# Second MoE of a fused attention and two-MoE kernel: the input-side products on two PSUM banks, zeroed by writing, one output sum in their upper halves

## Chip, cores and metric

One NeuronCore of a Trainium2 chip runs the whole program in one launch. The metric is the device time of an execution in microseconds (us). Five engines work side by side and meet only through semaphores: TensorE (PE) multiplies, VectorE (DVE) and ScalarE (ACT) do element-wise work and read PSUM, GpSimd (POOL) does element-wise work between SBUF tiles, and SyncE (SP) issues the DMAs. PSUM, into which PE writes, has eight banks; a tile of 128 x 512 fp32 values fills one.

## The reference, cut to what matters

```python
scores = q @ k.T * scale                      # 4 x 8 heads, 576 x 576
attn = softmax(where(scores >= max - tau, scores, -1e9))
x = (attn @ v), heads side by side            # 2304 x 512
h = x @ w1_in                                 # 512 -> 2048
x = (h * clip(h + 3, 0, 6) / 6) @ w1_out      # first MoE, 2048 -> 512
h = x @ w2_in
out = (h * sigmoid(1.702 * h)) @ w2_out       # second MoE
```

## The kernel before

The program keeps tokens on the free axis and features on partitions. Every fp32 operand is split into two numbers of a shorter format, a high and a low one, and a product is three matmuls: high by high, high by low, low by high. Attention and the first MoE come first (to about 659 us of the profiled execution), then the second MoE, which is where the diff works.

**The second MoE.** `moe2` (L1368) takes a block of 512 tokens (four of them) or of 256 (one, called `whole`). The feed-forward width is cut into eight pairs of 128 x 2; two sweeps (`q` = 0, 1) take four pairs each over all blocks, the first sweep storing its sums in DRAM, the second adding to them. One block and one pair are called a step here: 40 steps, 32 of them with 512 tokens. A step of 512 tokens uses a 2 x 2 scheme with seven products in place of eight, on the input side (`hidden2`, L1251, matmuls at L1269) and on the output side (`yout` and `prod` in `moe2`, matmuls at L1395). One product is six matmuls with 256 columns. A step of 256 tokens has four products on each side.

- Input side: the seven products go to the two 256-column halves of one PSUM bank (`ps`, class 3 of `bank`, of which one may be open). Each half is a running sum that is never started anew within the step; after some products ACT copies the running value out (`kept`: tiles p1, p5, u2 and half of b) or DVE adds it to such a copy (`plus`). The two results a and b (128 x 512 each) are made of these and one subtraction between SBUF tiles (`TC`, on DVE or POOL).
- Between: `gate2` (L1313) applies a sigmoid on ACT (L1338), a multiplication on DVE, four differences, and splits the results into high and low parts (ACT copies, then differences on DVE or POOL: tiles g and gl).
- Output side: the seven products of a step add to seven sums that live over the four pairs of a sweep; four of them are the `py` banks and three are banks of `pm`, class 4. At the end of a block the sums are combined on DVE and POOL and stored.

The order of all instructions is not the order of the code. `Plan` collects operations with their costs; `order` (L221) schedules them by a table of ranks (`RANKS`), with the number of open banks per class in `CAPS`, and another table (`SWAPS`) says which operations with two possible engines take the second one. Each engine then runs its instructions in that order. A wait is made wherever two instructions touch the same tile. In the time that the plan leaves PE idle, `fill` (L361) puts matmuls on a constant tile (`busy`, L1566).

Lines in the profile: L507 is the ACT copy helper, L510 the two-input element-wise helper on DVE or POOL, so those are told apart by their tiles. `pm` is any of the four banks of that pool, `xhxs`/`xlxs` and many `inhring`, `outhring` tiles hold activations.

Of the kernel before, what the change touches and what calls it, by code (L numbers as in the profile page):

```python
# [15 lines left out]
ALU = mybir.AluOpType  # L16
# [15 lines left out]
CAPS, BANKS, LANES = (2, 2, 3, 1, 3), 4, 8  # L32
# [4 lines left out]
3jhuP4gnqk3IJLFM*sx^J^|nXq5)0;9RmFU0s%PzegQB6H~|s?t^qs&YynFFR{>K2K>;cOi~)23QUOT;ZUJ%uX8~9ND*?~}DFHwMpaEI|NCDab`vHvsf&pFulL1Tt6afYS!U049M*-piv;k=W(g8{V8UcU-Q3A68s{vF2`~l7Z;{h20?*WPd  # L37
p8}`>uK_gzsR4!o3IYoPdjZS=RsjS8K?3Lj_W^4GSOV|?g8{4oA_8UtSpl#CrvZEc8UmyNhXD}+B?9&V>H$jvTLJ<C5&}B{6#{btVFGXhtO9QWS^`G`Ujj@57y>H-b^?L|4FV(rRswPY1_EFL2m;pu3<Ko?ya53M+XC1DECQ_ofdTgb^#NZ2
+yVaqnF3+~kpT|@-~iSD*Z__I3;`wqNdou)mH@5*p8$;jSpYczdI1pu@&V=m(E!c>#Q>-Ph5&s47XY6D3;+cHwE!gnZUAQh9RL~t0RU(Khyi8+Z2^4&cmbIKj{#)?i2(or8vrf<2>=5CCID3cNdQ~`H2?wtBLG+c761qU9{_X!e*l00PXH$X
TLCcuVF7Xg$N+}`<Nz`N`~Y15gaMTSAOgw(k^vk6w*lV)bpgEr-T|fo=>Y%%WC1n-&jA4e4FLlI%>X|ER{}%=2?EgpodMJVJp!BojsXM!sQ}*qaR6fgGyqEg!vH}5Isj7u-2k!xwg8d<Bmf}*EdVS45&+r&Kmy?akO86q%>j=9xB*rGE&|X1  # L40
# [6 lines left out]
C<CDa76VuVTLY&8q66v!DFinIaRXHY&;ykN&jYpt<O96}=L2*E$^(}J^aBb62L#Cj_XBtXCIrp{3k2H)W(1!EF$5k2e*~BWR0L53ZUlS;_5-~HV+6Paf&?D~X9TeXfCRe*O9k-+t^_Uwa|Db8sRVuor34cN00p)LmIQbNVg#KAItA_oHw8om
T?H5g!UQ}82L%QNs07&r%><MLTm|?FV+$Dz(ggklV+Aq={RBk?Z3RLFItywG{t9;mqXmKmg$0QP?FDWH<OOXDmkc`#u?2$#(FJ=2D+Uh+M+S}s><U5)WD86KWCFzjQUd(~+W~F@jRNljr~)ekz5>VsGy<3c$OF;>aRT!KmI7S@GXwquZ~zbl
#sa(oP67-9YXkHGpaVJs4g-?|dIKK=`2uYN+W<TRO#_1mIRo<mu>&Fln+5U$R0C)OGy}8)cLUi2U;~8%rUP;V#{+u<M+1ukz5|W}m;>$u5d^aX#{otI>H_})_yR)%`~q+T*aA2MNCSBTAOnp9N&`*<^8>;Ir31ACfdktE*#M^lsRMljqysJk
fCFO#ECYuFh65l3W&@l9g9E<<Zvz4ZngbdHMFT7Zr~~2yKm;TNp##GM@&nWZVgr!_mIDt3*aX%D-2?&!9tHUX>;xbMQUxsoDFeU)4+A>``U2(x4FgL96a!rYSpzBq1p`R~ZUYwsbpyKtuLHFN-vep`4+J&?90Q&MUIX0&%>&B=?E{hn-~-hI  # L50
90bt=c?7ZpsspD4gacs%w*ycEF9eJO1O(Ru^#khz1q8VR`UB$wH3TaJ83afKCj^oNJ_Jt$RRp&LWdtJxy9DV2>;otS{{zGW7X;`7Lj<q`I|PUW!2{9*lmm$bnFHnnhXhFkFa!exiv+j>aRlT9TLggwJp<kYX#@ZSpafO~6a+T}Jp@Mtn*^Bz
lLU1H#sqc*&jeWn`UI;4qy)eNQUrzs)CAlF2?RU@X9d&+>;+W?{RNE$Uj?BBs|BD1`va>3Uju&wj|2Dv76e8FdIVkseFQ25Oaxj4d;>ECT?BFjO9UkZ;RG86f&(-J76niQ8w9EZZv?Ugkpy1^;{-VbIs`ifjRfrkAq1iXU<8i@a0EmIECmb&
=md@gVFbwpx&+q*Aq5Bp$^@JQWCYU$^#m6M`vgY?Fa<pYZv|NeKLs%b`~$oM9R=b9Qv`PeDg`11Y6MCIgapF`Nd@)<1_Xly{{&VAv;^=390gznA_RT}k_8n6G6X*aZ3ImO4Ft>sQv)yqQUeVIB?a^Z5(H5N;RA{VN(FQUCj}4%Qw1gkfCUu=
X$AKLe+4!LF9qublLg@g00zDV=>^CI3kIMDG6xt0bOX!;djyaK<pekc-vsysXaqC`4h16x#01C$?*u3Xzy#(5vjn6CSOrc5g#=dx+5`&)odog(DFx&L9RunF^8`!<Km{2EwFLtO5e47`qXYy6CIi9(MFc_wuLAr8K?Ga`p#*jXl?A2*#{{ec
5(Pm8=LAp%O$EjUWd#8Rlm#;dcm;?Az69$8bp^!(z5#gwiUeu_E&;;=?g5knS_1_E@dNM!uLR2k&;+mqVg>R5;sEXd?*ME7_5i;C=m6>fi~vIbGXUHGi33{ziUW86S_O6hvjs5$Bn4>z><9D!aRCYgx&=Q2mIXcq`T%nPssPLe9|u+kcK}xa
X$SrWss<<rPyjmt5CNM3+XZL_j|Hj)-UJ2)`2}?b%mtkVzy;C;odW>`Q3gT==LP5mdIlc`Mh1iiJqAGr9tQjctp)G}7zQ#15e6Fut_2eYzXntWBnFTMX$HXtuLa=-Rt9(m3<g97QU){z0tO)lBL-&%KnA1+bOwJ0Wd_Lxe+QxlZU!y}lm=V|
# [325 lines left out]
def tile_top_attention_moe_moe2(  # L382
# [76 lines left out]
    def buf(tag, ring, pool, shape, dt=F32):  # L459
        return Buf(pl, tag, ring, lambda: pools[pool].tile(shape, dt, tag=tag, name=tag, bufs=ring), pool)  # L460
# [743 lines left out]
    def halves(c0, n, whole, K):  # L1204
# [425 lines left out]
```

## Time and profile before

| | |
|---|---|
| median of 3 runs | 1101.16 us (1095.71 to 1102.01) |
| the profiled execution: its own time | 1096.64 us |
| its span | 1094.8 us |
| busy over the span: PE, weight loads, DVE, ACT, POOL | 95%, 87%, 83%, 60%, 49% |

The profile is of one execution. Its engines' busy times overlap. A matmul's duration includes its way through the array, so the next one starts before the last has ended, and PE's pace is read from the distance between starts. An idle time is named by what ended it.

### The profile page before, as it was taken

Reading aid. Unit: us, or ns where it says so; the run is one execution under the profiler, and the core shown is the slowest. Engines: PE = TensorE matmul, PEld = TensorE weight load, DVE = VectorE, ACT = ScalarE, POOL = GpSimd, SP = SyncE. Lnnn points to the kernel's source line nnn. Section 1 sums busy time; section 2 is a strip of 40 time slices with the busy share of each in tenths; the row PEclk is TensorE's granted clock in tenths of the full one; section 3 lists DMA queues with packets and bytes.
Section 4 is the critical chain, followed back from the end, with each engine's and each line's share of the span. In section 5 each row is a group of like instructions: output and inputs, shape, how many; then the busy total and the mean of one; then the engine's idle time right before and its main releaser. Section 6 shows DMA issues by size and latency. Waiting matters only on the chain.

```text
span 1094.8 us, 21058 instructions
## 1 busy us (share of the span) xinstructions
PE 1038.8 (95%) x7564; PEld 956.1 (87%) x7564; DVE 905.3 (83%) x1845; ACT 653.8 (60%) x1307; POOL 536.3 (49%) x641
## 2 busy tenths in 40 slices
PE   8999999999999999999999998999999879888998
PEld 6687878899988889999999997988988878888898
DVE  7999999988998957878878776777898999778865
ACT  5898776767776646664544445555556845444452
POOL 3688887866485626554653433343423121433332
PEclk9999999999999999999999999999999999999999
DMA  7334457777866654456458772142315631211202
GB/s 233 106 111 144 143 160 221 201 196 197 247 204 189 177 163 131 146 189 197 142 171 285 224 254 82 49 150 83 107 44 183 217 110 46 78 58 59 87 11 78
DMA packets 98633, 160.70 MB, mean 147 GB/s; under 512 B 9056, under 2 KB 61408, under 8 KB 96480
## 3 DMA queue, kind: packets, MB, share of 16 engines
q1 hardware_dynamic: 98384, 159.06, 47.9%
q8 instruction: 60, 0.98, 0.4%
q14 instruction: 45, 0.37, 0.1%
q10 hardware_dynamic: 144, 0.29, 0.1%
HBM read 106.76 MB, written 52.56 MB: 146 GB/s over the span
## 4 chain that ended last, share of the span: by engine, by line
PE 72%; DVE 12%; DMA 6%; ACT 5%; issue 3%; POOL 2%; SPq 1%; DVEq 0%; ACTq 0%; POOLq 0%
PE pm L1269 15%; PE py L1073 8%; PE py L1395 8%; PE pm L1048 8%; PE pm L1163 6%; PE pm L1073 5%; PE ps L768 5%; PE pm L1395 4%; PE pm L986 4%; PE pm L894 3%; DVE c L510 2%; PE pm L970 2%; DMA wrawstg<-in_w1o_dram 2%; PE ps L808 1%; ACT p L507 1%
## 5 line engine op out<-in xcount | busy, mean ns | idle before, releaser
L824 DVE TENSOR_REDUCE nm<-ps 128x1 f32<-128x576 f32 x144 | 105.6, 748 | 16.6 <-PE ps L768 12.0
L507 ACT ACTIVATE g<-t 128x256 fp32r<-128x256 f32 (+3 forms) x178 | 86.4, 489 | 44.2 <-DVE t L510 20.3
L827 ACT ACTIVATE e<-ps,nm 128x576 f32<-128x576 f32 x128 | 92.4, 736 | 28.6 <-DVE nm L824 24.1
L1073 PE MATMUL pm<-g,outhring 128*128 128x256 f32 (+1 forms) x512 | 106.4, 300 | 0.0
L828 DVE SCALAR_TENSOR_TENSOR e<-ps,th,e 128x576 f32<-128x576 f32 x128 | 102.0, 809 | 3.8 <-ACT e L827 1.9
L1073 PE MATMUL py<-g,outhring 128*128 128x432 f32 (+2 forms) x384 | 97.1, 337 | 1.8 <-DVE yc L510 1.0
L510 POOL TENSOR_TENSOR g<-t,g 128x256 fp32r<-128x256 f32 (+2 forms) x74 | 66.4, 898 | 66.0 <-ACT g L507 44.8
L1048 PE MATMUL pm<-xh,inhring 128*128 128x256 f32 (+1 forms) x320 | 96.9, 303 | 0.4 <-DVE t L1060 0.3
L1048 PE MATMUL pm<-xh,inlring 128*128 128x256 f32 (+1 forms) x320 | 94.6, 296 | 0.0
L1048 PE MATMUL pm<-xl,inhring 128*128 128x256 f32 (+1 forms) x320 | 94.5, 295 | 0.0
L768 PE MATMUL ps<-kqv 128*128 128x288 f32 x480 | 81.6, 302 | 1.2 <-DVE kqv L510 0.5
L1073 PEld LDWEIGHTS pm<-g,outhring 128*128 128x128 f32 x512 | 82.0, 190 | 0.6 <-issue 0.5
L510 POOL TENSOR_TENSOR wmstg<-wmstg,wrstg 128x512 uint32<-128x512 uint32 x40 | 55.1, 1380 | 53.1 <-DVE wmstg L564 39.8
L1073 PE MATMUL pm<-g,outlring 128*128 128x256 f32 (+1 forms) x256 | 75.9, 297 | 0.0
L768 PEld LDWEIGHTS ps<-kqv 128*128 128x128 f32 x480 | 68.4, 190 | 8.0 <-issue 3.9
L1073 PEld LDWEIGHTS py<-g,outhring 128*128 128x128 f32 x384 | 68.6, 188 | 4.2 <-DVE yc L510 1.2
L510 DVE TENSOR_TENSOR t<-t,c 128x512 f32<-128x512 f32 (+1 forms) x80 | 57.3, 723 | 16.3 <-ACT t L1338 15.7
L510 DVE TENSOR_TENSOR g<-t,g 128x256 fp32r<-128x256 f32 (+2 forms) x86 | 52.2, 610 | 15.2 <-ACT g L507 14.5
L1073 PE MATMUL py<-g,outlring 128*128 128x432 f32 (+2 forms) x192 | 64.7, 337 | 0.0
L510 POOL TENSOR_TENSOR kqv<-qk,kqv 64x576 fp32r<-64x576 f32 (+1 forms) x40 | 57.8, 1444 | 11.7 <-ACT kqv L507 4.7
L897 ACT ACTIVATE et<-pm 128x512 f32<-128x512 f32 (+2 forms) x102 | 55.2, 557 | 13.5 <-PE pm L894 12.6
L1048 PEld LDWEIGHTS pm<-xh,inhring 128*128 128x128 f32 x320 | 60.6, 189 | 1.1 <-PE pm L1571 0.5
(245 smaller groups left out, 3704.4 us busy)
## 6 DMA issues: line engine op xcount, KB each, us to landing
turned<-tr SPq DMA_DIRECT2D x16, 1024.0 KB, 4.4
et<-turned SPq DMA_DIRECT2D x64, 256.0 KB, 5.6
wrawstg<-in_w1i_dram SPq DMA_DIRECT2D x16, 512.0 KB, 4.0
wrawstg<-in_w1o_dram SPq DMA_DIRECT2D x16, 512.0 KB, 3.7
wrawstg<-in_w2i_dram SPq DMA_DIRECT2D x16, 512.0 KB, 4.3
wrawstg<-in_w2o_dram SPq DMA_DIRECT2D x16, 512.0 KB, 4.4
qk<-in_q_dram SPq DMA_DIRECT2D x24, 288.0 KB, 4.5
qk<-in_k_dram SPq DMA_DIRECT2D x24, 288.0 KB, 4.2
```

What stands on the lines that cost most here:

```text
L507: return lambda: nc.scalar.activation(out=o(), in_=i(), func=ACTF.Copy, **kw)
L510: return lambda: (nc.vector if eng == DVE else nc.gpsimd).tensor_tensor(out=o(), in0=a(), in1=b(), op=op)
L768: nc.tensor.matmul(ps.t[:, i, :SH], q, w[hd].t[:, i * SH:(i + 1) * SH], start=a, stop=z)
L824: add(DVE, 672, K("R", s), "R", lambda: nc.vector.tensor_reduce(out=nm.t[:, c], in_=ps.t[:, :, :SH], op=ALU.max, axis=AX.XY, negate=True), ...
L827: add(ACT, 624, K("X", s), "X", lambda: nc.scalar.activation(out=ev(), in_=ps.t[:, :, :SH], func=ACTF.Exp, bias=nm.t[:, c]), [ps, (nm, s)] ...
L828: add(DVE, 736, K("M", s), "M", lambda: nc.vector.scalar_tensor_tensor(out=ev(), in0=ps.t[:, :, :SH], scalar=th.t[:, c], in1=ev(), op0=ALU ...
L897: add(ACT, act(size), K("EH", at), "EH", lambda: nc.scalar.activation(out=dst()[0], in_=dst()[1](pt.t[row:kn, :size]), func=ACTF.Copy), [p ...
L1048: nc.tensor.matmul(ph.t[:, :n], a, v, start=(cc == 0 and i == 0), stop=(cc == KC - 1 and i == 2))
L1073: nc.tensor.matmul(py.t[:, :n], a, v, start=(st and i == 0), stop=(sp and i == 2))
L1163: nc.tensor.matmul(ph.t[:, :n], a, v, start=(cc == 0 and q == 0), stop=(cc == KC - 1 and q == 2))
L1269: nc.tensor.matmul(half(i)(), u.t[:, ws], v.t[:, xv], start=(st and kk == 0 and j == 0), stop=(sp and kk == 1 and j == 2), skip_group_chec ...
L1395: nc.tensor.matmul(o.t[:, cc * n:cc * n + n], u.t[:, ws], v.t[:, at:at + n], start=(st and j == 0 and cc == 0), stop=(sp and j == 2), skip ...
```

## The change

Two banks of `pm` are taken for good at the start of the second MoE (`pab`). Each holds, in its lower 256 columns, one of the two running places of the input side, and in its upper 256 columns half of the output sum of product (0, 0). No matmul into these banks sets the start flag; instead ACT writes zeros (`zero`: an identity tile times 0.0), over both banks once, over both lower halves after each step (40 steps, 80 writes), and over both upper halves at the end of each 512-token block (16 writes). `CAPS` lets two banks of class 3 be open and two of class 4, in place of one and three.

Inside a step the seven products alternate between the banks, in another order, and the sums are put together another way: four copies, three additions or subtractions from PSUM and now two between SBUF tiles (`side`, on DVE or POOL) in place of one. The copy of the (0, 0) output sum (512 columns) becomes two copies of 256, one from each bank. In the output products of a step (0, 0) now comes last, except in a block's last step.

`buf` gives each place of a ring its own tag and one buffer, where one tag had as many buffers as the ring has places. `RANKS` and `SWAPS` are other tables: the whole program, attention and first MoE included, is ordered anew, and some operations change engine.

```diff
-CAPS, BANKS, LANES = (2, 2, 3, 1, 3), 4, 8
+CAPS, BANKS, LANES = (2, 2, 3, 2, 2), 4, 8
...
-    23, 42, 72, 185, 212, 247, 274, 316, 350, 383, 393, 398, 429, 495, 617, 651, 661, 669, 705, 715, 737, 745, 761, 814, 825, 846, 876, 910, 932, 949, 967, 968, 972, 997, 1002, 1008,
+    62, 72, 102, 212, 226, 247, 254, 274, 298, 309, 371, 378, 388, 398, 422, 538, 551, 617, 647, 667, 786, 793, 794, 825, 856, 885, 910, 915, 920, 925, 928, 937, 947, 953, 972, 1002,
...
-        return Buf(pl, tag, ring, lambda: pools[pool].tile(shape, dt, tag=tag, name=tag, bufs=ring), pool)
+        b = Buf(pl, tag, ring, None, pool)
+        b.make = lambda: pools[pool].tile(shape, dt, tag=f"{tag}{b.idx % ring}" if ring > 1 else tag, name=tag, bufs=1)
+        return b
...
-        ps = bank(3)
...
-            return lambda: ps.t[:, 256 * i:256 * i + n]
+            return lambda: pab[i].t[:, :n]
...
-                        nc.tensor.matmul(half(i)(), u.t[:, ws], v.t[:, xv], start=(st and kk == 0 and j == 0), stop=(sp and kk == 1 and j == 2), skip_group_check=True)
+                        nc.tensor.matmul(half(i)(), u.t[:, ws], v.t[:, xv], start=False, stop=True, skip_group_check=True)
...
+        def side(o, x, y, op, rd, wr):
+            add(DVE, dve(n), K("H2") + 4500, "TC", tt(DVE, o, x, y, op), rd, [wr], (), (POOL, pool2(n), tt(POOL, o, x, y, op)))
...
-        prod(1, (4, 1), False, False)
-        kept(first(p5), 1, [p5])
-        prod(0, (5, 3), False, False)
-        kept(first(u2), 0, [u2])
-        prod(1, (2, 4), False, True)
-        plus(a, second(a), 1, u2, 1)
-        prod(0, (6, 5), False, False)
-        plus(b, second(b), 0, p5, 1)
-        prod(0, (3, 6), False, False)
-        kept(first(b), 0, [(b, 0)])
...
-        prod(0, (1, 2), False, True)
-        plus(a, first(a), 0, p1, 0)
...
+            prod(1, (1, 2))
+            kept(first(a), 1, (a, 0))
+            prod(0, (5, 3))
+            kept(first(u2), 0, u2)
+            prod(1, (4, 1))
+            comb(first(p5), 1, (first(a), (a, 0)), ALU.subtract, p5)
+            prod(0, (6, 5))
+            comb(second(b), 0, (first(p5), p5), ALU.add, (b, 1))
+            side(first(u2), first(u2), first(a), ALU.subtract, [(a, 0)], u2)
+            prod(1, (2, 4))
+            comb(second(a), 1, (first(u2), u2), ALU.add, (a, 1))
+            prod(0, (3, 6))
+            kept(first(b), 0, (b, 0))
+            side(first(a), first(a), first(p1), ALU.add, [p1], (a, 0))
+        for i in range(2):
+            zero(i, 0, n, K("H2") + 5000)
...
+        return add(ACT, act(n), time, "Z", lambda: nc.scalar.activation(out=ap(), in_=id_b.t.unsqueeze(1).to_broadcast([P, n // P, P]), func=ACTF.Copy, scale=0.0), [id_b], [pab[i]])
...
-        accs += [bank(4) for _ in range(0 if whole else 3)]
+        accs = accs if whole else [None] + accs + [bank(4) for _ in range(2)]
...
+                    to = o.t[:, cc * n:cc * n + n] if o else pab[cc].t[:, 256:512]
...
-            for q in place:
+            for q in place if whole or i == len(w) - 1 else [*list(place)[1:], (0, 0)]:
...
+        def open_():
+            for i in range(2):
+                add(ACT, act(n), t, "KP", copy(lambda i=i: side(u)()[:, i * n:i * n + n], lambda i=i: pab[i].t[:, 256:512]), [pab[i]], [u])
+                zero(i, 256, n, t)
...
+    pab += [bank(3) for _ in range(2)]
+    for i in range(2):
+        zero(i, 0, 512, t - 10000).deps.add(changed[-2][0])
```

In the built programs PE has 7112 matmuls before and after, SP 543 instructions, DVE 1703; ACT goes from 1310 to 1442 and POOL from 646 to 652.

PE's order in the second MoE, first step of the third block worked on, at the border of two input-side products (last three matmuls of one, first three of the next; the number behind `pm` tells the tile). Before:

```order
L1269 MATMUL pm_9244<-xhxs_8404,inhring1_6632 128x256
L1269 MATMUL pm_9244<-xlxs_8415,inhring1_6632 128x256
L1269 MATMUL pm_9244<-xhxs_8404,inlring1_6643 128x256
L1269 MATMUL pm_9244<-xhxs_8420,inhring1_6762 128x256
L1269 MATMUL pm_9244<-xlxs_8446,inhring1_6762 128x256
L1269 MATMUL pm_9244<-xhxs_8420,inlring1_6777 128x256
```

PE's order there now:

```order
L1271 MATMUL pm_8359<-xhxs_8398,inhring1_6637 128x256
L1271 MATMUL pm_8359<-xlxs_8419,inhring1_6637 128x256
L1271 MATMUL pm_8359<-xhxs_8398,inlring1_6648 128x256
L1271 MATMUL pm_8365<-xhxs_8409,inhring1_6732 128x256
L1271 MATMUL pm_8365<-xlxs_8420,inhring1_6732 128x256
L1271 MATMUL pm_8365<-xhxs_8409,inlring1_6755 128x256
```

Both products wrote one tile; now each writes its own.

ACT's order in the same step (copies out of `pm` into p, u, c; `g` are high parts of the gate, `t` its sigmoid). Before:

```order
L507 ACTIVATE p_9263<-pm 128x256
L507 ACTIVATE g<-t_861 128x256
L507 ACTIVATE p_9273<-pm 128x256
L507 ACTIVATE u_9283<-pm 128x256
L507 ACTIVATE wrstg_9304<-wrawstg_9240 128x512
L507 ACTIVATE yc<-py_9054 128x512
L507 ACTIVATE c<-pm 128x256
```

ACT's order there now, where `pm<-id` is a zero:

```order
L510 ACTIVATE c<-pm 128x256
L510 ACTIVATE g<-t_936 128x256
L510 ACTIVATE p_9273<-pm 128x256
L510 ACTIVATE g<-t_888 128x256
L510 ACTIVATE u_9291<-pm 128x256
L510 ACTIVATE wrstg_9320<-wrawstg_9242 128x512
L1323 ACTIVATE pm<-id 128x256
L510 ACTIVATE c<-pm 128x256
L1350 ACTIVATE t_888<-c 128x512
L1323 ACTIVATE pm<-id 128x256
```

The four copies of a step stay; two zeros have come in among them and the sigmoids.

## Rows read from the trace of the kernel before

**Rows 1.** The page: busy time by engine, and PE's granted clock in 40 slices.
```profile
PE 1038.8 (95%) x7564; PEld 956.1 (87%) x7564; DVE 905.3 (83%) x1845; ACT 653.8 (60%) x1307; POOL 536.3 (49%) x641
...
PEclk9999999999999999999999999999999999999999
```

**Rows 2.** Busy time by stage: stretch, length, then each engine's busy us.
```profile
0.00:659.00 659.00, 648.11 (x4482) 585.02 (x4483) 559.94 (x1227) 425.05 (x827) 395.66 (x524) 1.00 0.62 185
659.00:1091.00 432.00, 390.68 (x3084) 371.03 (x3082) 344.71 (x619) 228.80 (x481) 140.62 (x117) 1.00 0.28 89
```

**Rows 3.** A group at L1269: ns min/median/max, first and last start.
```profile
L1269 PE MATMUL pm<-inhring,inhring x72: 275/282/392, 659.1 to 1043.4; 128*128 128x256 f32 x72
```

**Rows 4.** A group at L1395, same columns.
```profile
L1395 PE MATMUL py<-g,outlring x160: 276/280/288, 685.0 to 1090.6; 128*128 128x256 f32 x160
```

**Rows 5.** PE's waits from 640 us on: us in total, times, longest.
```profile
PE pm L1269 <- ACT p L507: 17.2, 33, 1.2
PE pm L1269 <- ACT u L507: 9.2, 19, 0.6
PE pm L1269 <- DVE c L510: 7.9, 11, 2.0
PE pm L1269 <- ACT c L507: 1.8, 5, 0.5
```

**Rows 6.** Timeline of PE, five input-side products: first matmul of each.
```profile
726.70 0.28 PE L1269 MATMUL pm<-xhxs,inhring 128*128 128x256 f32 x1
...
727.41 0.28 PE L1269 MATMUL pm<-xhxs,inhring 128*128 128x256 f32 x1
...
728.00 0.28 PE L1269 MATMUL pm<-xhxs,inlring 128*128 128x256 f32 x1
728.75 0.39 PE L1269 MATMUL pm<-inhring,inhring 128*128 128x256 f32 x1 [0.47 <-ACT p L507]
...
730.19 0.39 PE L1269 MATMUL pm<-outhring,inhring 128*128 128x256 f32 x1 [0.47 <-ACT p L507]
...
731.64 0.39 PE L1269 MATMUL pm<-inhring,inhring 128*128 128x256 f32 x1 [0.47 <-ACT u L507]
```

**Rows 7.** Timeline of ACT over the same products: its copies out of that bank.
```profile
728.32 0.38 ACT L507 ACTIVATE p<-pm 128x256 f32<-128x256 f32 x1 [0.47 <-PE pm L1269]
...
729.75 0.38 ACT L507 ACTIVATE p<-pm 128x256 f32<-128x256 f32 x1 [0.75 <-PE pm L1269]
731.20 0.38 ACT L507 ACTIVATE u<-pm 128x256 f32<-128x256 f32 x1 [1.06 <-PE pm L1269]
```

**Rows 8.** Groups on ACT in the second MoE, by shape.
```profile
L507 ACT ACTIVATE p<-pm 128x256 f32<-128x256 f32 x72 | 27.0, 381 | 41.6 <-PE pm L1269 41.4
...
L1338 ACT ACTIVATE t<-c 128x256 f32<-128x256 f32 x16 | 6.7, 416 | 9.5 <-DVE c L510 8.8 <-DVE g L510 0.5
```

**Rows 9.** Groups on DVE in the second MoE, by shape.
```profile
L510 DVE TENSOR_TENSOR gl<-c,g 128x512 fp32r<-128x512 f32 x42 | 33.0, 789 | 1.5 <-ACT g L507 0.7 <-PE pm L1395 0.5
...
L510 DVE TENSOR_TENSOR c<-t,c 128x256 f32<-128x256 f32 x49 | 23.4, 477 | 1.1 <-POOL c L510 1.0
L510 DVE TENSOR_TENSOR g<-t,g 128x256 fp32r<-128x256 f32 x35 | 20.1, 575 | 9.3 <-ACT g L507 9.0
...
L510 DVE TENSOR_TENSOR yc<-yc,wrawstg 128x512 f32<-128x512 f32 x10 | 8.5, 849 | 0.1
```

**Rows 10.** Busy time by stretch inside the second MoE.
```profile
780.00:960.00 180.00, 159.06 (x1241) 149.69 (x1240) 159.52 (x291) 101.56 (x211) 49.12 (x39) 1.00 0.35 113
840.00:900.00 60.00, 49.34 (x378) 45.68 (x377) 55.78 (x103) 37.70 (x79) 12.16 (x9) 1.00 0.52 168
```

**Rows 11.** Timeline of DVE, two operations with two SBUF inputs.
```profile
703.48 0.96 DVE L510 TENSOR_TENSOR g<-t,g 128x256 fp32r<-128x256 f32 x1
704.36 0.41 DVE L510 TENSOR_TENSOR c<-t,t 128x256 f32<-128x256 f32 x1
```

**Rows 12.** Timeline of POOL in the same stretch.
```profile
703.03 1.12 POOL L510 TENSOR_TENSOR c<-t 128x256 f32<-128x256 f32 x1 [0.63 <-DVE t L510]
704.49 1.43 POOL L510 TENSOR_TENSOR xlxs<-xa,xhxs 128x512 fp32r<-128x512 f32 x1 [0.34 <-ACT xhxs L507]
```

More of the change, by code (lines that the diff above doesn't have):

```diff
@@ L1279, in second, with comb @@
             return lambda: x.t[:, n:2 * n]
-        def plus(t, o, i, y, reg):
-            add(DVE, dve(n), K("H2") + 4000, "U", tt(DVE, o, half(i), first(y), ALU.add), [(ps, i), y], [(t, reg)])
+        def comb(o, i, y, op, wr):
+            add(DVE, dve(n), K("H2") + 4000, "U", tt(DVE, o, half(i), y[0], op), [pab[i], y[1]], [wr])
         def kept(o, i, wr):
-            add(ACT, act(n), K("H2") + 1000, "KP", copy(o, half(i)), [(ps, i)], wr)
-        prod(0, (0, 0), True, False)
-        kept(first(p1), 0, [p1])
@@ L1302, in hidden2 @@
-        plus(a, second(a), 1, u2, 1)
-        prod(0, (6, 5), False, False)
-        plus(b, second(b), 0, p5, 1)
-        prod(0, (3, 6), False, False)
-        kept(first(b), 0, [(b, 0)])
-        sides = [first(p1), first(p1), first(b)]
-        add(DVE, dve(n), K("H2") + 4500, "TC", tt(DVE, *sides, ALU.subtract), [(b, 0)], [p1], (), (POOL, pool2(n), tt(POOL, *sides, ALU.subtract)))
-        prod(0, (1, 2), False, True)
-        plus(a, first(a), 0, p1, 0)
+            add(ACT, act(n), K("H2") + 1000, "KP", copy(o, half(i)), [pab[i]], [wr])
@@ new lines, in side @@
+        def side(o, x, y, op, rd, wr):
+            add(DVE, dve(n), K("H2") + 4500, "TC", tt(DVE, o, x, y, op), rd, [wr], (), (POOL, pool2(n), tt(POOL, o, x, y, op)))
+        prod(0, (0, 0))
+        kept(first(p1), 0, p1)
+        if whole:
+            prod(1, (6, 0))
+            prod(1, (3, 1))
+            comb(first(b), 1, (first(p1), p1), ALU.add, (b, 0))
+            prod(0, (1, 1))
+            kept(first(a), 0, (a, 0))
+        else:
+            p5, u2 = buf("p5", 1, "ct", [P, 256]), buf("u2", 1, "ct", [P, 256])
+            prod(1, (1, 2))
[12 more added lines that the diff above has]
+            side(first(a), first(a), first(p1), ALU.add, [p1], (a, 0))
@@ L1393, in mm @@
                     ws = slice(lo + cc * P, lo + cc * P + P)
+                    to = o.t[:, cc * n:cc * n + n] if o else pab[cc].t[:, 256:512]
                     for j, (u, v, at) in enumerate(((wh, gh, ho), (wh, gl, go), (wl, gh, ho))):
[L1395 to L1397 removed]
+                        nc.tensor.matmul(to, u.t[:, ws], v.t[:, at:at + n], start=(st and j == 0 and cc == 0 and o is not None), stop=(sp and j == 2), skip_group_check=True)
+            add(PE, 6 * pe(n), K("Y", i + 1) + 640 * list(place).index(q), "Y", mm, [(wh, reg), (wl, reg), (gh, hr), (gl, lr)], [o] if o else list(pab))
         def yout(i, g):
[L1400 removed]
+            for q in place if whole or i == len(w) - 1 else [*list(place)[1:], (0, 0)]:
                 prod(i, q, g, place[q], i == 0 and q != (3, 1) if whole else i == 0, i == len(w) - 1 and q != (6, 0) if whole else i == len(w) - 1)
@@ L1457, in moe2 @@
             u, v = (uv, 0), (uv, 1)
+        def open_():
+            for i in range(2):
+                add(ACT, act(n), t, "KP", copy(lambda i=i: side(u)()[:, i * n:i * n + n], lambda i=i: pab[i].t[:, 256:512]), [pab[i]], [u])
+                zero(i, 256, n, t)
         if first:
-            add(ACT, act(2 * n), t, "KP", copy(side(u), side(a1)), [a1], [u])
+            open_()
             plus(y11, a2, u)
@@ L1467, in moe2 @@
         else:
-            add(ACT, act(2 * n), t, "KP", copy(side(u), side(a1)), [a1], [u])
+            open_()
             onto(y11, u)
```

206 lines of the change are left out of this document (100 added, 106 removed), and 23 rows, old and new, of the table SWAPS.

## The prediction

> **What bounds the kernel now.** I read the page first, then busy time by stage, then PE's waits, then timelines of single products, and last the groups by shape on DVE and ACT.
>
> PE is busy 95% of the span at a granted clock of nine tenths or more in every slice, the 2.4 GHz level [rows 1]; the question is where the rest goes. By stage [rows 2], the 659 us of attention and first MoE hold 648 us of PE work: 11 us are idle. The second MoE, from 659 to 1091 us, holds 391 of 432, and "busy" flatters it, since a matmul counts its 0.28 us while the next may start after 0.12. So take starts: the input-side and output-side products run from 659.1 [rows 3] to 1090.6 + 0.28 [rows 4], 431.8 us. There are 512 products (32 steps of 14, 8 of 8). In flow one takes 0.71 us (726.70 to 727.41) [rows 6], so all take 363.5. About 68 us are lost.
>
> PE's waits name the place [rows 5]: 33 + 19 + 11 + 5 = 68 waits of input-side products for a copy or an addition that reads their bank, 36.1 us idle. The timelines show what one is. Products start at 728.75, 730.19 and 731.64 [rows 6], 1.44 us apart where flow is 0.71. ACT's copy for the product of 726.70, all of which was issued when the next began at 727.41, starts only at 728.32 [rows 7]: 0.04 us after the end (728.00 + 0.28) of the product that followed it into the other half of the same bank. So a copy waits for whatever was last issued into the bank, and the next product waits for the copy. The halves give no overlap; only another bank would. One such turnaround costs 1.44 - 0.71 = 0.73 us, of which the row shows 0.47 as idle. So the 68 waits cost 36.1 + 68 x 0.26 = 53.8 us.
>
> **The change part by part.**
>
> *Turnarounds removed.* I count, in the built order, how many products stand between the last product in a bank ahead of a read and the next product in that bank. Before, 51 of 256 input-side products have none between; now 4. Before, 48 products wait for two reads in a row on one bank; now none. The 51 cost 51 x 0.73 = 37.2 us. The other 16.6 of 53.8 belong to pairs of reads and to DVE additions that come late; the ends are that none or all of it goes, and I take half, 8.3, because the pairs go and DVE's queue gets no shorter. With one product between, a single read is covered: 0.71 us against 0.73.
>
> *Turnarounds added.* A zero is an ACT instruction of 256 columns behind the read. The trace has no write of ACT to PSUM; the nearest rows are 0.381 us for the copy out of PSUM and 0.416 for SBUF to SBUF of that size [rows 8]. It is work added, so not below nothing. I take 0.381, the row with PSUM at one end, and 0.05 for the hand-over, the gap from the copy's end at 728.70 to the matmul at 728.75. Read and zero take 0.73 + 0.43 = 1.16 us. Two products cover that; one leaves 0.45. The order has 46 products behind a zero: 2 with no product between, 5 with one, 39 with two or more. So 4 x 0.73 + 2 x 0.43 + 5 x 0.45 = 6.0 us. On PE alone the balance is -37.2 - 8.3 + 6.0 = -39.5 us.
>
> *ACT's load.* 96 zeros x 0.381 = 36.6 us, two wide ones and the split copies some 3 us: from 229 to 268 of about 410 us. ACT's idle time hides that. What it could cost is order: a zero waits for the last read of its bank, in 40 steps a DVE addition, and behind it on ACT stand sigmoids and gate copies, which DVE and then the output-side products wait for. The ends are nothing and 40 x 0.48 = 19 us (one addition each) [rows 9]; I take nothing, since the order has one or more output-side products ready there.
>
> *DVE's load.* In the second MoE DVE gets 33 instructions more: 38 more of 256 columns between SBUF tiles (mean 0.477), 6 more of the kind yc<-yc,wrawstg (0.849), 3 fewer g<-t,g (0.575), 4 fewer gl<-c,g (0.789) [rows 9], and four small ones fewer (2 us): 18.1 + 5.1 - 1.7 - 3.2 - 2 = 16.3 us. DVE rises from 344.7 [rows 2] to 361. POOL loses as much as it gains. This decides how much of PE's gain stays. From 780 to 960 us DVE is busy 159.5 of 180 us, and the fullest 60 us have 55.8, 93% [rows 10]. With its share of the extra, 6.8, that stretch needs 166.3 / 0.93 = 178.8 us: of PE's 16.5 us there (180/432 of 39.5) only 1.2 stay. In the other 252 us DVE has 185.2 + 9.5 = 194.7 us of work, 85% of the 229 left after PE's 23.0 us: those stay. Together -24.2 us.
>
> The 0.477 is a mean over pieces of two prices: g<-t,g took 0.96 us beside a POOL operation and c<-t,t 0.41 before the next one began [rows 11, 12]. For the 38 the ends are therefore 15.6 and 36.5 us; I keep the mean, because POOL's load in this stage does not change.
>
> The Trainium skill speaks against this part: GPSIMD Engine Reference, section Specifications, says that GpSimd shares its SBUF interfaces with VectorE and contends with DVE instructions that have two SBUF inputs, and the 38 are such, where the additions from PSUM have one. The two rows just named agree with it. If every added one met POOL, the rule would make 18 us of 36.5 the extra, 7.6 of it in the full stretch, and the time some 8 us more.
>
> *Nothing or not known.* Fixed ring places add no instruction, and neither does the missing start flag. The matmuls (7112) and SP's instructions (543) are as many as before; SP and ACT's DMA queue are only reordered. In the first stage the new order takes 33 instructions from DVE and gives 26 to ACT, 7 to POOL. PE's idle time there is 11 us, so at best a few go, and a worse order could add as many: -5 to +5, taken as 0.
>
> The sum: the profiled execution's own time 1096.64 (1.8 around its span), less 24.2: 1072.4. The median of the runs shown, 1101.16, is 4.5 above that execution, whose time lies at the low end of them; I forecast 1072.
>
> **The rivals.**
>
> *PE alone decides.* If DVE can be filled beyond 93%, all 39.5 us stay: 1057; with the rest of the late reads and a better first stage 1044. For it: much of DVE's idle time ends with PE's products. Against: no stretch of before shows such a share.
>
> *The wait moves to the zeros.* Each step now begins behind two zeros. If ACT reaches them so late that one product per step has the whole turnaround before it, 40 x 0.73 = 29 us come back: 1072 + 29 = 1101, no change. It decides from the point where a zero starts more than two products (1.42 us) after its bank's last product. For it: ACT's g copies of 0.4 to 0.6 us stand in the same queue. Against: ACT is idle 203 of 432 us.
>
> *DVE sets the pace (slower).* If DVE's 87 us of idle time in this stage come from the chain sigmoid, product, differences, gate parts, and not from PE, its share stays 344.7 / 432 = 80%, and 361 us need 452: +20, 1117. It decides where DVE's added differences come ahead of work that PE waits for. For it: DVE is at 89% in the middle. Against: 57 of PE's 68 waits are for ACT's copies [rows 5].
>
> *The change does not do what it says.* If a copy waited for the next product whatever its bank, the turnarounds would stay and only work be added: also no change or slower. The copy at 728.32 beginning on the end of a product in its own bank speaks against it.
>
> **How the numbers follow.** The forecast (1061 to 1086) has 0.55, PE alone (1044 to 1061) 0.22, no change by the zeros or by banks 0.16, slower 0.07. What a measurement of this kernel can tell from no change is about 1%, 11 us around the median of 1101: faster is 0.78, within 0.15, slower 0.07. The range leaves out about a tenth at each side: 1048 to 1096.
>
> **What would show it.** Right: PE's waits for copies of p, u and c shrink from 68 to about a dozen; consecutive input-side products start 0.71 us apart; a new ACT group pm<-id of 96 with some 0.38 us; DVE's share of the second MoE near 88%, its length near 408 us. Wrong: PE waiting for zeros by tens of microseconds; products still 1.44 us apart; DVE's share as it was; or a first stage whose length moves by more than 5 us.

## The result and the profile after

| | before | after |
|---|---|---|
| median (runs in one comparison) | 1101.2 us (4 runs, 1095.71 to 1102.01) | 1069.11 us (4 runs, 1066.28 to 1072.01) |
| ratio, 95% interval | | 0.9719, 0.9674 to 0.9764 |
| profiled execution, its span | 1096.64, 1094.8 us | 1071.15, 1069.3 us |
| first input-side product to start of the last output-side one | 659.1 to 1090.6 us | 659.8 to 1065.1 us |

The kernel is 2.8% faster; 1072 was forecast. The page shows it with the same 7564 matmul records, PE busier and more work on DVE and ACT than its 905.3 and 653.8 us of before [rows 1]. The lines are busy time by engine and PE's granted clock in 40 slices:

```profile
PE 1033.4 (97%) x7564; PEld 957.6 (90%) x7564; DVE 916.0 (86%) x1845; ACT 689.1 (64%) x1439; POOL 571.7 (53%) x647
...
PEclk9999999999999999999999999999999989999999
```

The groups that answer to [rows 3, 4] give the ends of the second MoE, at L1271 and L1408 now. It begins 0.7 us later and is 26.2 us shorter (431.5 to 405.3, start to start):

```profile
L1271 PE MATMUL pm<-inhring,inhring x72: 276/282/386, 659.8 to 1021.0; 128*128 128x256 f32 x72
```
```profile
L1408 PE MATMUL py<-g,outlring x160: 276/279/287, 686.7 to 1065.1; 128*128 128x256 f32 x160
```

PE's waits from 640 us on answer to [rows 5] (columns: us in total, times, longest):

```profile
PE pm L1271 <- DVE p L513: 7.0, 5, 3.2
PE pm L1271 <- ACT pm L1323: 4.8, 5, 1.4
PE py L1408 <- DVE gl L513: 2.0, 4, 0.7
PE pm L1271 <- DVE c L513: 1.7, 5, 0.9
PE pm L1271 <- ACT p L510: 1.1, 2, 0.6
PE pm L1271 <- ACT c L510: 1.1, 2, 0.6
```

Of 57 waits for ACT's copies (p, u, c) five are left, one of them for u and short. What is late now are additions of DVE (p, c: 10 times, 8.7 us) and zeros (5 times, 4.8 us). The timelines show why. Three input-side products follow one another on PE, the first matmul of each:

```profile
725.33 0.28 PE L1271 MATMUL pm<-xhxs,inhring 128*128 128x256 f32 x1
...
726.02 0.28 PE L1271 MATMUL pm<-xhxs,inhring 128*128 128x256 f32 x1
...
726.72 0.38 PE L1271 MATMUL pm<-inhring,inhring 128*128 128x256 f32 x1
```

and ACT in the same stretch:

```profile
726.28 0.39 ACT L510 ACTIVATE p<-pm 128x256 f32<-128x256 f32 x1 [0.53 <-PE pm L1271]
```

The product of 725.33 has issued its last matmul at 725.91, which ends at 726.19. The copy starts at 726.28, in the middle of the next product, which goes to the other bank. It ends at 726.67, and the third product, back in the first bank, starts at 726.72: no idle time, but only just. Starts are 0.69 and 0.70 us apart, where [rows 6] had 1.44.

The groups on ACT and DVE in the second MoE answer to [rows 8, 9], the windows to [rows 2, 10]:

```profile
L1323 ACT ACTIVATE pm<-id 128x256 f32<-128x256 f32 x96 | 36.4, 382 | 37.0 <-DVE c L513 36.0
```
```profile
L513 DVE TENSOR_TENSOR gl<-c,g 128x512 fp32r<-128x512 f32 x39 | 28.9, 740 | 2.2 <-ACT g L510 1.0 <-PE py L1408 0.9
L513 DVE TENSOR_TENSOR c<-t,c 128x256 f32<-128x256 f32 x55 | 28.7, 523 | 0.2
L513 DVE TENSOR_TENSOR u<-u,c 128x256 f32<-128x256 f32 x24 | 13.2, 549 | 3.2 <-ACT u L510 3.0
L513 DVE TENSOR_TENSOR yc<-yc,wrawstg 128x512 f32<-128x512 f32 x16 | 11.8, 740 | 2.7 <-ACT wrawstg L510 2.7
```
```profile
659.00:1066.00 407.00, 386.67 (x3100) 377.02 (x3098) 355.12 (x658) 256.56 (x587) 160.50 (x116) 0.98 0.30 96
780.00:960.00 180.00, 164.69 (x1285) 159.28 (x1284) 169.71 (x318) 116.22 (x259) 65.01 (x37) 0.96 0.35 112
840.00:900.00 60.00, 52.45 (x396) 50.13 (x395) 57.61 (x107) 41.46 (x93) 18.36 (x9) 0.94 0.49 157
```

DVE holds 355.12 of 407 us; in the middle 169.71 of 180 (94%), and 57.61 of 60 (96%) where before had 55.78. To place a gain or a loss, the starts of the 512 products were read from each trace. Products 0 to 127, 128 to 255, 256 to 287 and 288 to 511 took, in us, up to the start of the last matmul (the runs behind the first two columns are those of the next section; after_again is the changed kernel measured once more, relieved leaves out what the three runs with no_ leave out singly). The last line is the time of this stage that TensorE spent at half its clock:

| products | before | after | after_again | no_zeros | two_zeros | no_side | no_wd | wd_pool | relieved |
|---|---|---|---|---|---|---|---|---|---|
| 0 to 127 | 107.7 | 101.8 | 101.5 | 100.6 | 109.5 | 101.6 | 102.2 | 102.1 | 99.8 |
| 128 to 255 | 104.4 | 103.5 | 103.5 | 99.2 | 107.6 | 99.4 | 101.8 | 103.0 | 99.2 |
| 256 to 287 | 33.0 | 33.0 | 33.1 | 31.7 | 30.5 | 28.1 | 26.2 | 37.2 | 25.5 |
| 288 to 511 | 186.4 | 167.0 | 163.8 | 163.9 | 177.8 | 168.8 | 165.6 | 163.9 | 163.1 |
| at half clock | 0 | 13.7 | 10.2 | 3.4 | 13.7 | 3.4 | 3.4 | 6.8 | 0 |

From product 128 to 287, about 767 to 900 us, the change won 0.9 us; all else came before and behind. In after, two of its three stretches at half the clock lie there; by the price that the last section works out they cost at most some 4 us (18 + 25 matmuls x 0.096).

### The profile page after: what moved, and what is told of

Its sections match the earlier page's. It is cut to its first block, busy times and chain, and to the rows that moved or that the text cites. A ratio compares the mean times of both kernels' runs of the same rounds, so it can differ in the third digit from the quotient of the medians.

```text
span 1069.3 us, 21238 instructions
## 1 busy us (share of the span) xinstructions
PE 1033.4 (97%) x7564; PEld 957.6 (90%) x7564; DVE 916.0 (86%) x1845; ACT 689.1 (64%) x1439; POOL 571.7 (53%) x647
## 4 chain that ended last, share of the span: by engine, by line
PE 61%; DVE 17%; DMA 7%; ACT 5%; issue 5%; POOL 3%; SPq 1%; DVEq 0%; ACTq 0%; POOLq 0%
PE pm L1271 13%; PE py L1408 7%; PE pm L1076 7%; PE py L1076 6%; PE pm L1166 6%; PE pm L1408 5%; PE ps L771 4%; PE pm L1051 4%; PE pm L989 4%; DVE c L513 3%; PE pm L897 2%; DMA wrawstg<-in_w1i_dram 2%; DMA wrawstg<-in_w1o_dram 2%; DVE nm L827 1%; DVE g L513 1%
## 5 line engine op out<-in xcount | busy, mean ns | idle before, releaser
L513 POOL TENSOR_TENSOR g<-t,g 128x256 fp32r<-128x256 f32 (+2 forms) x93 | 87.4, 945 | 116.1 <-ACT g L510 71.6
L510 ACT ACTIVATE g<-t 128x256 fp32r<-128x256 f32 (+3 forms) x188 | 90.2, 487 | 48.8 <-DVE t L1178 21.3
L513 POOL TENSOR_TENSOR gl<-c,g 128x512 fp32r<-128x512 f32 x25 | 50.5, 2021 | 56.7 <-ACT g L510 24.0
L513 DVE TENSOR_TENSOR t<-t,c 128x512 f32<-128x512 f32 (+1 forms) x80 | 55.7, 705 | 18.1 <-ACT t L1350 17.5
L513 POOL TENSOR_TENSOR kqv<-qk,kqv 64x576 fp32r<-64x576 f32 (+1 forms) x42 | 61.0, 1452 | 11.2 <-ACT kqv L510 4.1
L1323 ACT ACTIVATE pm<-id 128x256 f32<-128x256 f32 (+1 forms) x98 | 37.5, 387 | 37.0 <-DVE c L513 36.0
```

The source lines that it names most:

```text
L510: return lambda: nc.scalar.activation(out=o(), in_=i(), func=ACTF.Copy, **kw)
L513: return lambda: (nc.vector if eng == DVE else nc.gpsimd).tensor_tensor(out=o(), in0=a(), in1=b(), op=op)
```

## The experiments

My theory is that of the prediction: a reader of a bank waits for the last product issued into it, so two banks remove turnarounds; DVE keeps the middle; zeros cost little. The rivals are that the new tables made the gain, that ACT behind the zeros sets the pace, and that DVE has slack.

**One bank again.** The order and the instructions of after, but both running places in the halves of one bank and the halves of the output sum in the other.

```diff
-            return lambda: pab[i].t[:, :n]
+            return lambda: pab[0].t[:, 256 * i:256 * i + n]
...
-                    to = o.t[:, cc * n:cc * n + n] if o else pab[cc].t[:, 256:512]
+                    to = o.t[:, cc * n:cc * n + n] if o else pab[1].t[:, cc * 256:cc * 256 + 256]
...
-                add(ACT, act(n), t, "KP", copy(lambda i=i: side(u)()[:, i * n:i * n + n], lambda i=i: pab[i].t[:, 256:512]), [pab[i]], [u])
+                add(ACT, act(n), t, "KP", copy(lambda i=i: side(u)()[:, i * n:i * n + n], lambda i=i: pab[1].t[:, i * 256:i * 256 + 256]), [pab[i]], [u])
```

(`zero` writes the places accordingly.)

> The changed kernel with its order, instructions and zeros as they are; only the places in PSUM differ: both running places of the input side lie in the halves of one bank, and the two halves of the (0, 0) output sum in the other. Theory (what was won are turnarounds inside a bank): in the order 43 products now stand directly behind the last product ahead of their read (4 in the changed kernel) and 56 more have one product between and two reads to wait for, so 39 x 0.73 + 56 x 0.45 = 54 us of PE time come back, less what DVE's full stretch hides: 1105 to 1125 us, no better than before. Rival (the new tables or the ring places won it): 1069 us, within 5.

Measured: 1143.3 us (1140.22 to 1145.45), ratio to before 1.0396 (1.0368 to 1.0424): 74 us above after, far more than I expected. PE's waits of this run:

```profile
PE pm L1271 <- ACT p L510: 12.6, 22, 1.2
PE pm L1271 <- DVE c L513: 10.3, 18, 1.4
PE pm L1271 <- ACT u L510: 9.8, 20, 2.0
PE pm L1271 <- ACT c L510: 9.3, 17, 1.0
PE pm L1271 <- ACT pm L1323: 8.8, 13, 1.0
PE pm L1271 <- DVE p L513: 6.6, 9, 2.8
```

They are 99 waits with 57.4 us of idle time, against the 19 with 15.7 us listed for after on the same tiles. With the 0.26 us that each hides, the prediction's price gives 41.7 + 80 x 0.26 = 62.5 of the 74 us. The separate banks are the mechanism. An order that alternates between two places relies on them: in one bank it makes more turnarounds than the order of before had. Here and in before the wait is the program's own, made wherever two instructions touch one tile, and a tile is a bank; whether the memory would allow a read of one half beside a write of the other was not tried.

**Fixed ring places alone**, in the kernel before:

```diff
-        return Buf(pl, tag, ring, lambda: pools[pool].tile(shape, dt, tag=tag, name=tag, bufs=ring), pool)
+        b = Buf(pl, tag, ring, None, pool)
+        b.make = lambda: pools[pool].tile(shape, dt, tag=f"{tag}{b.idx % ring}" if ring > 1 else tag, name=tag, bufs=1)
+        return b
```

> The kernel before with fixed ring places and nothing else. Theory: no change, 1101 us within 6, since it adds and removes no instruction. Rival (the ring places gave a part of the gain by other waits): 1069 to 1090 us.

Measured: 1099.48 us, ratio 1.0005 (0.9984 to 1.0026). This part of the change does nothing for the time.

**Structure or tables.** Both kernels with the two tables emptied, so that the planner's own rules order them.

```diff
-RANKS = """
...
+RANKS = """"""
...
-SWAPS = (
...
+SWAPS = ()
```

> The kernel before, with its two tables of numbers (priorities and swaps of neighbours) emptied, so that the planner's own rules set the order. It is the base of the next run. Both theories expect it slower than the kernel before, by 1 to 8%: 1112 to 1190 us.

> The changed kernel with both tables emptied: structure alone, since the order now follows from the same rules in both. If the second bank itself removes the turnarounds, this is 1.5 to 4% faster than the run without tables before it. Rival: the new tables made the gain, and the structure, with its 96 zeros, is worth nothing by itself: within 1% of it or slower.

Measured: 1136.53 us (1135.15 to 1138.54) and 1101.3 us (1098.17 to 1105.43), a quotient of 0.969, beside 0.972 with the tables. In the traces the second MoE takes 446.6 and 420.3 us, 26.3 less; with the tables it was 26.2 less. PE's waits there for ACT's copies go from 43 of 22.5 us to 6 of 4.2 us. So the structure gives the gain without the tables too. That the two agree to 0.1 us is chance: the traces without tables hold 17 and 20 us at half the clock, before none and after 13.7. Without tables the first stage is 7.0 us shorter too (684.5 to 677.5 us), for a cause that I did not look for.

**The zeros left out, and written twice.**

```diff
-        return add(ACT, act(n), time, "Z", lambda: nc.scalar.activation(out=ap(), in_=id_b.t.unsqueeze(1).to_broadcast([P, n // P, P]), func=ACTF.Copy, scale=0.0), [id_b], [pab[i]])
+        return add(ACT, act(n), time, "Z", (lambda: nc.scalar.activation(out=ap(), in_=id_b.t.unsqueeze(1).to_broadcast([P, n // P, P]), func=ACTF.Copy, scale=0.0)) if n > 256 else (lambda: None), [id_b], [pab[i]])
```

> The changed kernel without the 96 zeros after steps and blocks (the two first ones stay), so its sums run on and the output is not the reference's. Theory (zeros cost little): PE's waits for zeros are 5.1 us in the changed kernel's trace, ACT has 151 us idle in this stage: 1060 to 1068 us. Rival (a good part of the wait moved to the zeros): 1050 us or less.

Measured: 1060.11 us (1058.84 to 1061.62), 9.0 below after and 8.0 below its second measurement. For the other direction each zero was issued twice in a row:

```diff
+        def write():
+            for _ in range(2):
+                nc.scalar.activation(out=ap(), in_=id_b.t.unsqueeze(1).to_broadcast([P, n // P, P]), func=ACTF.Copy, scale=0.0)
...
+        return add(ACT, act(n), time, "Z", write, [id_b], [pab[i]])
```

> The changed kernel with each of the 96 zeros written twice in a row: ACT has 37 us more, about 294 of 407 us in the second MoE. If a zero costs only where few products stand between it and the next product of its bank (7 of 46 have none or one), every such place gets 0.39 us longer and the whole is 3 to 9 us slower, 1072 to 1078. Rival 1, ACT's idle time hides all of it: 1066 to 1071. Rival 2, ACT's queue is what sets the pace behind the zeros (sigmoids and gate copies come late): over 12 us slower, above 1081.

Measured: 1092.0 us (1090.02 to 1095.26), 23 above after. My theory said 3 to 9: it fell, and hidden ACT work fell with it. The waits for zeros in the run with two (L1325 is the zero; the second line is of output-side products into the same banks):

```profile
PE pm L1271 <- ACT pm L1325: 12.0, 16, 2.2
PE pm L1412 <- ACT pm L1325: 6.1, 15, 0.8
```

31 waits of 18.1 us stand against 6 of 5.1 us in after. The 25 new ones explain 13.0 us plus 25 x 0.26 = 6.5 of the 23. So PE waits for the zero itself, not for the sigmoids behind it on ACT: its waits for parts of the gate (g, gl) are 2.4 us in after and 2.9 here. In some 25 places of 96 an extra 0.39 us is enough to be seen. What makes such a zero late is mostly what ACT runs ahead of it. The group above has 36.0 of the 37.0 us that ACT idles ahead of zeros end with a DVE addition (c), but the zeros that PE waits for are others: in after all six follow another ACT instruction with at most 0.03 us of idle time, three a copy out of PSUM, two a sigmoid, one a copy of activations. One of them, on ACT and then on PE:

```profile
857.06 0.36 ACT L510 ACTIVATE yc<-pm 128x256 f32<-128x256 f32 x1
857.32 0.62 ACT L1350 ACTIVATE t<-c 128x512 f32<-128x512 f32 x1
857.84 0.37 ACT L1323 ACTIVATE pm<-id 128x256 f32<-128x256 f32 x1
```
```profile
858.27 0.39 PE L1271 MATMUL pm<-xhxs,inhring 128*128 128x256 f32 x1 [1.07 <-ACT pm L1323]
```

The copy, the last reader, ends at 857.42; the sigmoid stands between it and the zero, and PE goes on 0.06 us after the zero's end. In the run with two, 30 of the 31 waits are for a pair of zeros that follows another ACT instruction without a pause, in 15 cases a sigmoid or a copy between SBUF tiles. So rival 2, whose time came true, is right that ACT's queue sets the pace, though by what stands ahead of a zero and not behind it. That time was not in my count of products between.

**The additions between SBUF tiles left out** (`side`, 64 of them):

```diff
-            add(DVE, dve(n), K("H2") + 4500, "TC", tt(DVE, o, x, y, op), rd, [wr], (), (POOL, pool2(n), tt(POOL, o, x, y, op)))
+            add(DVE, dve(n), K("H2") + 4500, "TC", lambda: None, rd, [wr], (), (POOL, pool2(n), lambda: None))
```

> The changed kernel without the 64 additions and subtractions between SBUF tiles on the input side (46 on DVE, 18 on POOL), so the output is not the reference's. Theory (DVE sets the pace between 780 and 1020 us): 46 x 0.48 = 22 us less on DVE, some 13 of it in the full stretch: 1053 to 1062 us. Rival (PE, ACT or PE's clock set it, DVE's share is only high): 1066 to 1070 us.

Measured: 1063.69 us (1062.3 to 1064.65), 5.4 below after: between the two expectations. The table places 9.0 us of gain at products 128 to 287, and a loss of 1.8 behind them. The gain is where I had said that DVE is full, but smaller than full occupation would give, and up to 4 us of those 9.0 are clock: after's two low stretches there are absent here.

**The differences of fetched weights left out** (`fetch`, l minus h), all else in its place:

```diff
-            add(DVE, dve(DM), time, "WD", low(DVE), [h], [l], (), (POOL, pool2(DM), low(POOL)))
+            add(DVE, dve(DM), time, "WD", lambda: None, [h], [l], (), (POOL, pool2(DM), lambda: None))
```

> The changed kernel without the differences of the fetched weights (the low halves, written with l minus h): 38 instructions of DVE and 6 of POOL fewer, of which 31 of DVE (22.8 us) lie in the second MoE and 20 (14.5 us) between 840 and 900 us, where DVE is busy 96%. The outputs are not the reference's. All else keeps its order. If DVE sets the pace in the middle, the time falls by 8 to 15 us, to 1054 to 1061. Rival: DVE is busy there only in step with PE, and has slack: 1064 to 1070.

Measured: 1060.11 us (1058.01 to 1062.5), 9.0 below after, as expected of a DVE that sets the pace. The windows of this run:

```profile
780.00:840.00 60.00, 55.53 (x454) 53.94 (x453) 56.42 (x111) 40.59 (x89) 20.64 (x16) 1.00 0.39 126
840.00:900.00 60.00, 55.08 (x444) 52.76 (x442) 49.05 (x96) 45.47 (x102) 12.90 (x11) 1.00 0.48 157
```

Where 20 of them are gone, DVE drops from 57.61 to 49.05 us, and PE rises from 52.45 to 55.08. The table puts 6.8 us of the gain on products 256 to 287 alone: 32 products took 33.0 us before, 33.0 after, and 26.2 here. (After has lost some 2.4 us there to a lower clock, told in the last section; before and this run have not, so up to that much of the 6.8 is clock.) At these products PE waited in before 4.0 us for DVE's additions and 2.3 us for ACT's copies, in after 4.5 and 0.5 us: the bank took the copies off, the clock put about as much back, and DVE's part stayed.

**Ten of those differences moved to POOL**, in the same places of the order, beside a second measurement of after on the same chip. (The numbers are operations of the plan between about 850 and 950 us.)

```diff
+        for n in (5535, 5531, 5555, 5563, 5559, 5583, 5539, 5607, 5587, 5547):
+            self.ops[n].fn = self.ops[n].alt[2]
         return sorted(self.ops, key=lambda o: (self.start[o.n], o.n))
```

> The changed kernel as it is, as the base of the two runs behind it on the same chip: 1066 to 1072 us.

> The changed kernel with ten of the differences of fetched weights (128x512, some 0.70 us on DVE) of the stretch from about 850 to 950 us given to POOL, in the same places of the order: DVE has 7 us less there, POOL some 15 us more (1.5 to 1.6 us each by POOL's own few of that shape). If DVE's load alone holds that stretch, the time falls by 3 to 6 us. Rival: POOL's work lengthens DVE's beside it and comes late itself (the Trainium skill, GPSIMD Engine Reference, section Specifications, has the two engines share SBUF interfaces), and nothing is won: 1 us faster to 6 slower.

Measured: after 1068.16 us (1063.11 to 1073.87), with the ten on POOL 1072.66 us (1071.04 to 1074.26); the ratios to before are 0.9721 (0.9674 to 0.9769) and 0.9766 (0.9734 to 0.9797), whose intervals overlap: no gain, the rival. This had been the one edit meant to beat after. DVE's groups from 780 to 960 us, first of after's second measurement, then with ten differences on POOL:

```profile
L513 DVE TENSOR_TENSOR c<-t,c 128x256 f32<-128x256 f32 x28 | 12.7, 453 | 0.0
L513 DVE TENSOR_TENSOR outlring<-outlring,outhring 128x512 fp32r<-128x512 f32 x13 | 9.6, 765 | 0.0
L513 DVE TENSOR_TENSOR inlring<-inlring,inhring 128x512 fp32r<-128x512 f32 x14 | 9.4, 681 | 0.0
```
```profile
L515 DVE TENSOR_TENSOR c<-t,c 128x256 f32<-128x256 f32 x28 | 16.0, 572 | 0.0
L515 DVE TENSOR_TENSOR inlring<-inlring,inhring 128x512 fp32r<-128x512 f32 x11 | 9.7, 878 | 0.0
L515 DVE TENSOR_TENSOR outlring<-outlring,outhring 128x512 fp32r<-128x512 f32 x6 | 5.2, 863 | 0.0
```

The ten leave DVE, and its busy time stays (171.19 and 170.71 of these 180 us), because what is left gets longer: c<-t,c from 0.453 to 0.572 us, inlring from 0.681 to 0.878. POOL needs 1.46 to 1.55 us for each. The Trainium skill, GPSIMD Engine Reference, section Specifications, says that GpSimd shares its SBUF interfaces with VectorE and contends with VectorE's instructions that have two SBUF inputs; these two groups agree, and the run shows what it costs.

**All three left out at once** (zeros, additions between SBUF tiles, differences): the three edits above together.

> The changed kernel without the 96 zeros, without the 64 additions between SBUF tiles behind the products and without the differences of fetched weights, all three at once; the outputs are not the reference's, PE's order is the same. Singly they gave 9, 5 and 9 us. If each hides behind the others (one and the same idle time of PE), the three give 10 to 15 us together: 1054 to 1060. Rival: they are separate waits and add up, 20 us or more: 1040 to 1050; that is also what the rival of the prediction, PE alone decides, would come to.

Measured: 1052.41 us (1050.84 to 1053.64), 16.7 below after, where the single runs add up to 9.0 + 5.4 + 9.0 = 23.4. It lies between the expectations, somewhat nearer to the first. Whether the missing 6.7 us mean that the costs hide behind one another stays open, because each single gain also holds clock that after had lost (last line of the table). At 0.096 us for each matmul started in a low stretch (59 in after, 45 in after_again, 16 in each single run, none here), an estimate at most, the second MoE would be 5.8, 3.3 and 5.4 us shorter than after's singly, 14.6 in sum, and 12.1 with all three; against after_again 8.4 in sum and 10.1. By that the three mostly add up. The second MoE takes 387.6 us here, 43.9 less than before.

## Why the prediction was right, point by point

*A turnaround per direct successor, removed by another bank: right.* The waits for copies went from 57 to 5, those for DVE's additions stayed (11 of 7.9 us, 10 of 8.7), starts are 0.69 to 0.70 us apart across a copy, the pair without tables repeats the gain (26.3 and 26.2 us), and one bank brings all of it back and more.

*The balance of PE alone, -39.5 us: near in size, not measured.* It held -45.5 us of turnarounds and late reads and +6.0 for the zeros. The run relieved of zeros and of much DVE work is 43.9 us shorter in the second MoE, where without zeros -45.5 stood; neither its trace nor before's has a low clock. That run takes other work away too, and DVE may still hold it in places, so no run measures the term alone.

*The zeros: 6.0 on PE right in size, nothing on ACT wrong.* Of the group, 0.382 us was forecast as 0.381, and the idle room on ACT is there (busy 256.56 of 407 us). The six waits hold 5.1 + 6 x 0.26 = 6.7 us. Leaving the zeros out gave 8 to 9, part of it clock: after's two executions at a mean clock of 0.998 and 0.997 lie 6 to 7 us above that run's median. What failed is the nothing on ACT, and with it the step that two products cover a read and a zero, 1.16 of 1.42 us: a sigmoid or a copy of 0.6 us between the two uses up that margin. The error stayed small here; the doubled zeros show that it was luck by a few tenths of a microsecond per place.

*DVE's load, +16.3 us: too large.* It rose by 10.4, from 344.71 to 355.12. The pieces were priced by their mean of before, and some got cheaper: gl<-c,g 0.789 to 0.740, yc<-yc,wrawstg 0.849 to 0.740. c<-t,c went the other way, 0.477 to 0.523. Contention on the whole did not grow: of DVE's additions between SBUF tiles, 58 were longer than 0.68 us (512 columns) or 0.415 us (256) by over 0.06 us before, 40.0 us in sum, and 57 by 37.6 us after. So the 8 us that the Trainium skill's rule (the same section) would have added, had every new one met POOL, did not come. By that rule the trace shows single cases, below, and no more of them than before.

*DVE keeps the middle: right in kind, overdone in size.* I let 1.2 of 16.5 us stay between 780 and 960 us, because no stretch of before had DVE above 93%. After has 94% there and 96% at the fullest. Over products 128 to 351, about that stretch, the time went from 192.5 to 188.6 us, and to 185.5 in the second measurement: 3.9 to 7.0 us stayed. All low stretches of the clock in this stage lie there in both traces; with the 59 and 45 matmuls x 0.096 = 5.7 and 4.3 us that they cost at most, up to 9.6 and 11.3 would have stayed. A share seen in one trace is a floor for what an engine can reach, not its ceiling. That DVE is the holder is what the runs without its additions or differences show, at the very products that had not moved, where more came free than the clock accounts for (6.8 and 4.9 us against 2.4).

*The rest of the second MoE keeps 23.0 us: right.* 239.0 us went to 216.7, 22.3 less, and 22.6 in the second measurement.

*First stage and fixed places: nothing.* The second MoE began 0.7 us later, in the second measurement 1.3 earlier; the fixed places gave 1.0005.

The sum came out well partly by luck. By that estimate the middle would have kept some 8 to 10 us more than the 1.2, and the falls of the clock, for which the sum has no term, took 4 to 6 back. And the -24.2 was taken from the profiled execution, 4.5 us below the median: from median to median the gain is 32.1 us. Of the rivals, the one that bound a wait to the zeros had its mechanism right, since PE does wait for them, and late because of ACT's queue, but with 6 waits instead of 40. The profiled run also carries about 6 us of the clock, told below.

## What to carry to other kernels

Where a reader of PSUM waits for a bank, count how many products stand between the last write ahead of the read and the next write to that bank; halves of a bank add nothing to that count, a second bank does. A helper instruction behind such a read, like a written zero, belongs in the count together with what its own engine runs between the read and it, even if that engine is half idle. And before a full VectorE is relieved by GpSimd, look at the durations beside each other: work with two SBUF inputs can come back as longer instructions.

## What the runs showed of the hardware that I had not expected

*An instruction of POOL can hold DVE until its own end.* The longest stall of PE in after, 3.23 us, waits for p of DVE, which is busy without a gap. PE, DVE and POOL around it:

```profile
873.92 0.28 PE L1271 MATMUL pm<-xhxs,outlring 128*128 128x256 f32 x1
877.43 0.58 PE L1271 MATMUL pm<-outhring,outhring 128*128 128x256 f32 x1 [3.23 <-DVE p L513]
877.81 0.42 PE L1271 MATMUL pm<-outlring,outhring 128*128 128x256 f32 x1
878.03 0.42 PE L1271 MATMUL pm<-outhring,outlring 128*128 128x256 f32 x1
```
```profile
872.41 1.42 DVE L513 TENSOR_TENSOR u<-u,c 128x256 f32<-128x256 f32 x1
873.75 1.50 DVE L513 TENSOR_TENSOR c<-t 128x256 f32<-128x256 f32 x1
...
876.97 0.41 DVE L513 TENSOR_TENSOR p<-pm,c 128x256 f32<-128x256 f32 x1
```
```profile
870.08 3.46 POOL L513 TENSOR_TENSOR gl<-c,g 128x512 fp32r<-128x512 f32 x1 [4.21 <-DVE inlring L513]
873.50 1.45 POOL L513 TENSOR_TENSOR gl<-t,g 128x512 fp32r<-128x512 f32 x1
```

u<-u,c, one of the additions that the change put in, and c<-t took 1.42 and 1.50 us, where an operation of that size takes 0.41 (p<-pm,c, with one input from PSUM). They end 0.29 and 0.30 us after POOL's two. POOL's first one took 3.46 us while DVE was busy without a gap, the second 1.45; DVE's four instructions ahead of u<-u,c, beside POOL's first, kept their 0.68 us. So the loss goes both ways, and 2.1 us of PE's stall are the excess of two DVE instructions that ended with POOL's. The second measurement repeats it at the same place: 1.41 and 1.49 us, and a stall of 3.22.

*TensorE's granted clock falls for a few microseconds, in some executions.* The last two matmuls above take 0.42 us instead of 0.28. The windows of after (last three columns: granted clock, DMA share, GB/s):

```profile
805.00:808.40 3.40, 3.40 (x18) 3.40 (x18) 2.93 (x8) 1.40 (x3) 0.00 (x0) 0.53 0.31 116
876.00:882.80 6.80, 5.37 (x25) 5.37 (x26) 5.87 (x13) 1.42 (x4) 0.00 (x0) 0.53 0.18 53
911.00:914.40 3.40, 3.40 (x19) 3.40 (x19) 3.25 (x6) 1.14 (x3) 3.40 (x1) 0.56 0.24 48
```

Half the clock is the lower level, 1.2 GHz. Matmuls then start 0.213 us apart in the median (0.22 at 877.81 and 878.03) instead of 0.117, so these 62, of which 59 start in a low stretch, cost about 62 x 0.096 = 6 us, or less where PE would have waited anyway. Each fall began within 4 us of the beginning of a stall of PE (from one start to the next 2.1 us at 801.7, 3.5 at 873.9, 1.4 at 908.3 us). Before's profiled run had none, although it has stalls of 2.3 and 2.2 us (at 876.6 and 988.2 us). The kernel before with fixed ring places has the same two stalls, 2.3 us at 876.6 and 2.2 at 989.6, and its clock fell behind each, at 879.6 and 992.2. After's second measurement fell at the first two of after's places and not at the third. The runs of before vary in the same way: 1105.0 us at a mean clock of 0.989, 1095.3 to 1098.4 at 1.0. The four runs of after have 1066.3 and 1067.1 us at 0.998 and 0.997, 1071.2 and 1072.0 at 0.993 and 0.994. Its second measurement does not sort that way (1065.7 and 1073.9 at 0.994, 1070.6 at 0.997, 1063.1 at 0.998), so the clock is not all of the spread. The run without all three had clocks of 0.999 to 1.0. So a fall behind a stall of PE adds to what the stall costs, and part of what the runs with work left out gained is clock. What decides whether a stall brings a fall stays open; the same stall did and did not.
